# Query blocks of 512 columns with a 64-query remainder, in a relu²-attention and gated-FFN kernel

## Chip, cores and metric

The kernel runs on one core of one Trainium2 chip. The metric is device time in microseconds for one execution. Before the change the median of three runs is 1611.57 us (1611.5 to 1611.7).

## The reference

Four batches of 3136 rows go through an attention whose weights are the squared positive part of the scores, and then through a feed-forward block (FFN) with a three-tap convolution and a sigmoid gate. All arrays are float32; D is 256, the score depth 64, the hidden width 1024.

```python
scores = (1.0 / S) * z @ z.transpose(0, 2, 1)       # (4, 3136, 3136), symmetric
x = u * (np.maximum(scores, 0.0) ** 2 @ v)          # (4, 3136, 256)
h = np.maximum(x @ w_in, 0.0)                       # (4, 3136, 1024)
conv_out[:, t] = sum(conv_w[k] * hp[:, t + k] for k in range(3))   # hp: h with a zero row at each end
out = (h * sigmoid(conv_out)) @ w_out               # (4, 3136, 256)
```

## The kernel before

**Precision.** TensorE works on fp32r operands. To keep fp32 accuracy every operand is split into a rounded high part and the rest (hi and lo: `ah`/`al`, `vh`/`vl`, `gh`/`gl`, `xh`/`xl`, `wih`/`wil`, `woh`/`wol`). A product is three matmuls: lo weight by hi, hi weight by hi, hi weight by lo. For the scores hi and lo of 64 rows each fill the 128 rows of the array, so that two matmuls (`zhh` and `zll` against `zq`) do.

**Tiling.** A batch has 7 query blocks of `NB` = 448 columns (`QB` = 7), 28 blocks in all. The keys are 25 chunks of 128 rows (`NJ` = 25), the last of 64 rows. A block has 25 slots, one for each key chunk. In a slot `attend` (L348) issues 6 matmuls of 448 columns into two PSUM banks `av0` and `av1` (4 for the half chunk, the block's last slot), and `scores` (L256) 2 matmuls for a slot `LA` = 4 ahead. `relu`, `square`, `split_hi` and `split_lo` turn scores into `ah` and `al` on ScalarE and VectorE.

**Symmetry.** Scores of chunks that an earlier block has computed for other queries are not computed again. `part` (L279, GpSimd) and `spill` (L287) write them to DRAM as two halves of 16 bits; `fetch` (a transposing DMA on SyncE's queue) and `join` (L307, GpSimd) bring them back transposed. This replaces 277 of the 700 slots' scores.

**FFN.** After a block's attention `gate_x` (L367) takes `av0` and `av1` out of PSUM and multiplies by u, `split_x` makes hi and lo, and the FFN of that block runs inside the next block's slots, one of 8 hidden chunks every three or four slots (`FS`): 6 matmuls in (`ffn_in`), relu, three taps, sigmoid, gate and split on ScalarE, VectorE and GpSimd, and 6 matmuls out (`ffn_out`) some ten slots later. A block's last two output columns need the next block's first hidden row, so the tiles run one column late; `halo` carries two columns from block to block, and a batch's last block has 450 columns.

**Order.** The order on every engine is written out by hand: `ev[slot]` has six classes, and the loop at the end (L604) runs PRE, the attention's steps, POST, PE0, `attend`, `scores`, PE1. Tile releases make the semaphore waits. The last block's FFN has nothing beside it and has a schedule of its own (`T_S` to `T_L`, `last_block`, L564). The weights arrive as float64 and are turned to fp32 in blocks 0 to 2 (`prep_w`, mostly VectorE).

**PSUM** has 8 banks of 512 fp32 columns: `s` two, `ph` two, `av0`, `av1`, `o0`, `o1`. A query block of 448 leaves 64 columns of each empty.

Of the kernel before, what the change touches and what calls it, by code (L numbers as in the profile page):

```python
# [55 lines left out]
T_S, T_X = 3, 0  # L56
T_O = [1, 1, 2, 2, 3, 3, 4, 5]
T_C = [3, 3, 3, 1, 4, 2, 2, 0, 1]
T_H, T_L = "AAVAAVAA", "GVGVGVGV"


@with_exitstack
def kernel(
# [16 lines left out]
    NB = 448  # L80
    QB = S // NB
    NJ = (S + P - 1) // P
    HALF = S - (NJ - 1) * P
    NBLK = B * QB
# [5 lines left out]
    assert DC == 2 and KW == 3 and 2 * DQ == P and HALF == 64  # L90
# [20 lines left out]
    ent = [[entries(b, q) for q in range(QB)] for b in range(B)]
    assert all(e[-1] == (NJ - 1, False) for x in ent for e in x)
# [14 lines left out]
    halo = const.tile([P, FC, 2], F32, name="halo")  # L127
    ebias = const.tile([P, 1], F32, name="ebias")
# [11 lines left out]
    def load_z(b, q):  # L140
        t = wk.tile([P, NB], F32, tag="zt", name="zt")
        nc.sync.dma_start(out=t, in_=z[b, :, q * NB : (q + 1) * NB])
        zst[q] = t

    def prep_z(q):
        c, t = slice(q * NB, (q + 1) * NB), zst.pop(q)
        nc.scalar.copy(zhh[:, c], t)
        sub(nc.gpsimd, zll[:, c], t, zhh[:, c])
        if q == QB - 1:

            for x in (zhh, zll):
# [12 lines left out]
    def first_z():
        t, h = zst.pop(0), 256
        x = wk.tile([P, NB], F32R, tag="zq", name="zq")
        nc.scalar.copy(zhh[:, :NB], t)
        nc.scalar.copy(x[LO], t[LO])
        sub(nc.vector, x[HI], t[HI], zhh[HI, :NB])
        sub(nc.vector, zll[:, :h], t[:, :h], zhh[:, :h])  # L170
        sub(nc.gpsimd, zll[:, h:NB], t[:, h:], zhh[:, h:NB])
        zq[0] = x
# [83 lines left out]
    def scores(k):  # L256
# [10 lines left out]
        nc.tensor.matmul(s[:, :NB], lhsT=zhh[:, w], rhs=zq[blk], start=True, stop=False)  # L267
        nc.tensor.matmul(s[:, :NB], lhsT=zll[:, w], rhs=zq[blk], start=False, stop=True)  # L268
# [406 lines left out]
```

## Time and the profile before

| What | Value |
|---|---|
| median of the runs | 1611.57 us |
| the profiled execution: span, first to last instruction | 1609.6 us |
| TensorE matmul (PE) busy | 1582.4 us (98%), 7678 matmuls |
| weight loads (PEld) busy | 1437.5 us (89%) |
| ScalarE (ACT) busy | 1272.6 us (79%) |
| VectorE (DVE) busy | 1145.3 us (71%) |
| GpSimd (POOL) busy | 1100.5 us (68%) |
| granted TensorE clock, mean | 1.000 of full speed |
| DMA | 179.66 MB, mean 112 GB/s |

The page gives no time for the profiled execution other than its span; what lies around the span (launch and end) is the difference to the median, 2.0 us. Durations of matmuls overlap, because they are pipelined: a row's duration of 0.36 us is the way of one matmul through the array, and the pace is read from the starts. "Idle before" is the time an engine waited just ahead of a group, and the arrow names what ended it.

### The profile page before, as it was taken

Reading aid. Unit: us, or ns where it says so; the run is one execution under the profiler, and the core shown is the slowest. Engines: PE = TensorE matmul, PEld = TensorE weight load, DVE = VectorE, ACT = ScalarE, POOL = GpSimd, SP = SyncE. Lnnn points to the kernel's source line nnn. Section 1 sums busy time; section 2 is a strip of 40 time slices with the busy share of each in tenths; the row PEclk is TensorE's granted clock in tenths of the full one; section 3 lists DMA queues with packets and bytes.
Section 4 is the critical chain, followed back from the end, with each engine's and each line's share of the span. In section 5 each row is a group of like instructions: output and inputs, shape, how many; then the busy total and the mean of one; then the engine's idle time right before and its main releaser. Section 6 shows DMA issues by size and latency. Waiting matters only on the chain.

```text
span 1609.6 us, 24946 instructions
## 1 busy us (share of the span) xinstructions
PE 1582.4 (98%) x7678; PEld 1437.5 (89%) x7678; DVE 1145.3 (71%) x1933; ACT 1272.6 (79%) x2592; POOL 1100.5 (68%) x1451
## 2 busy tenths in 40 slices
PE   8899999999999999999999999999999999999998
PEld 7678999999999989999999998999999999999997
DVE  7897776667777777666777767766677777666656
ACT  8888777888877778788877777787887777787886
POOL 6775567787856667678785666777877566677772
PEclk9999999999999999999999999999999999999999
DMA  5342244555434434556453344445634334444450
GB/s 175 120 127 78 78 124 116 113 110 131 148 89 112 113 94 113 122 112 125 103 159 95 95 129 103 108 112 115 148 102 128 98 98 112 110 104 102 117 103 23
DMA packets 371399, 179.66 MB, mean 112 GB/s; under 512 B 264897, under 2 KB 370241, under 8 KB 371265
## 3 DMA queue, kind: packets, MB, share of 16 engines
q1 hardware_dynamic: 371120, 177.84, 44.3%
q8 instruction: 60, 0.98, 0.3%
q14 instruction: 75, 0.61, 0.1%
q10 hardware_dynamic: 144, 0.23, 0.0%
HBM read 36.59 MB, written 77.87 MB: 71 GB/s over the span
## 4 chain that ended last, share of the span: by engine, by line
PE 87%; ACT 5%; DVE 4%; issue 2%; POOL 2%; DMA 0%; POOLq 0%; ACTq 0%; DVEq 0%
PE av L358 15%; PE av L359 15%; PE av L360 15%; PE ph L393 5%; PE ph L391 5%; PE s L267 5%; PE ph L392 5%; PE o L460 5%; PE o L458 5%; PE o L459 5%; PE s L268 5%; DVE al L131 1%; ACT t L319 1%; ACT xh L381 1%; DVE ph L427 1%
## 5 line engine op out<-in xcount | busy, mean ns | idle before, releaser
L131 DVE TENSOR_TENSOR al<-s,ah 128x448 fp32r<-128x448 f32 x672 | 418.3, 622 | 238.5 <-ACT ah L335 163.0
L358 PE MATMUL av<-ah,vl 128*128 128x448 f32 x1344 | 492.7, 367 | 3.4 <-ACT ah L337 2.4
L360 PE MATMUL av<-al,vh 128*128 128x448 f32 x1344 | 491.7, 366 | 1.7 <-DVE al L131 1.4
L359 PE MATMUL av<-ah,vh 128*128 128x448 f32 x1344 | 492.3, 366 | 0.0
L330 DVE TENSOR_TENSOR s<-s,t 128x448 f32<-128x448 f32 x396 | 249.7, 630 | 205.2 <-ACT t L319 204.9
L311 POOL COPY tj<-tp 128x896 uint16<-128x896 uint16 x277 | 335.4, 1214 | 2.1 <-DMA tp<-dq 2.1
L319 ACT ACTIVATE t<-s 128x448 f32<-128x448 f32 x423 | 230.5, 545 | 116.8 <-PE s L268 106.4
L337 ACT CAST ah<-s 128x448 fp32r<-128x448 f32 x423 | 225.6, 533 | 112.0 <-DVE s L330 110.2
L427 DVE SCALAR_TENSOR_TENSOR ph<-hb,cw,ph 128x448 f32<-128x448 f32 (+1 forms) x448 | 304.8, 681 | 3.3 <-POOL gl L131 1.9
L131 POOL TENSOR_TENSOR gl<-c,gh 128x448 fp32r<-128x448 f32 (+1 forms) x220 | 255.6, 1162 | 67.9 <-ACT gh L134 63.2
L285 POOL COPY pl<-t 128x896 uint16<-128x896 uint16 x301 | 279.1, 936 | 1.4 <-ACT t L319 1.4
L358 PEld LDWEIGHTS av<-ah,vl 128*128 128x128 f32 x1344 | 252.6, 188 | 28.4 <-ACT ah L337 3.4
L360 PEld LDWEIGHTS av<-al,vh 128*128 128x128 f32 x1344 | 252.6, 188 | 25.5 <-DVE al L131 4.6
L359 PEld LDWEIGHTS av<-ah,vh 128*128 128x128 f32 x1344 | 252.7, 188 | 20.2
L416 POOL COPY halo<-hb 128x2 f32<-128x2 f32 x192 | 36.9, 192 | 291.0 <-ACT hb L414 290.9
L267 PE MATMUL s<-zq,zhh 128*128 128x448 f32 x423 | 160.3, 379 | 15.5 <-DVE al L131 8.7
L391 PE MATMUL ph<-xh,wih 128*128 128x448 f32 x448 | 164.3, 367 | 1.1 <-DVE c L441 0.7
L460 PE MATMUL o<-gl,woh 128*128 128x448 f32 (+1 forms) x448 | 164.1, 366 | 0.9 <-POOL gl L131 0.9
L393 PE MATMUL ph<-xl,wih 128*128 128x448 f32 x448 | 164.2, 367 | 0.3 <-POOL hb L405 0.3
L458 PE MATMUL o<-gh,wol 128*128 128x448 f32 (+1 forms) x448 | 164.3, 367 | 0.0
L459 PE MATMUL o<-gh,woh 128*128 128x448 f32 (+1 forms) x448 | 164.0, 366 | 0.0
L392 PE MATMUL ph<-xh,wil 128*128 128x448 f32 x448 | 163.7, 365 | 0.0
(78 smaller groups left out, 2370.5 us busy)
## 6 DMA issues: line engine op xcount, KB each, us to landing
dq<-pl SPq DMA_DIRECT2D x243, 224.0 KB, 2.3
ut<-in_u_dram SPq DMA_DIRECT2D x28, 448.0 KB, 3.8
vst<-in_v_dram SPq DMA_DIRECT2D x48, 256.0 KB, 3.1
dq<-pl SPq DMA_DIRECT2D x81, 112.0 KB, 2.4
out_dram<-ob SPq DMA_DIRECT2D x20, 448.0 KB, 3.3
zt<-in_z_dram SPq DMA_DIRECT2D x28, 224.0 KB, 3.1
tp<-dq SPq DMA_TRANSPOSE x277, 3.2
wr<-in_moe_w_in_dram SPq DMA_DIRECT2D x8, 256.0 KB, 3.2
```

The costliest lines, as they stand in the source:

```text
L131: eng.tensor_tensor(out=out, in0=a, in1=b.bitcast(F32), op=ALU.subtract)
L285: nc.gpsimd.tensor_copy(pl[k], rl.pop(k).bitcast(U16).rearrange("p (n h) -> p h n", h=2))
L311: nc.gpsimd.tensor_copy(tj[k].bitcast(U16).rearrange("p (n h) -> p h n", h=2), t)
L319: nc.scalar.activation(rl[k], sc[k][:, :NB], AF.Relu, scale=SC1)
L330: nc.vector.tensor_tensor(out=s, in0=s, in1=rl[k], op=ALU.mult)
L358: nc.tensor.matmul(o, lhsT=vl[:, j, d], rhs=h, start=first, stop=False)
L359: nc.tensor.matmul(o, lhsT=vh[:, j, d], rhs=h, start=False, stop=False)
L360: nc.tensor.matmul(o, lhsT=vh[:, j, d], rhs=l, start=False, stop=False)
L391: nc.tensor.matmul(o, lhsT=wih[:, dc, w], rhs=xh[blk][:, dc], start=(dc == 0), stop=False)
L393: nc.tensor.matmul(o, lhsT=wih[:, dc, w], rhs=xl[blk][:, dc], start=False, stop=(dc == DC - 1))
L427: nc.vector.scalar_tensor_tensor(out=c, in0=hb[blk, f][:, k : e + k], scalar=cw[:, f, k : k + 1], in1=c, op0=ALU.mult, op1=ALU.add,)
L458: nc.tensor.matmul(o, lhsT=wol[:, f, d], rhs=h, start=(f == 0), stop=False)
```

## The change

The query block becomes 512 columns, a whole PSUM bank. A batch then has 6 blocks (`QB` = 6) and 64 remaining queries (`RQ`), and the kernel 24 blocks.

- **The remainder's attention.** Hi and lo of 64 queries' attention weights stand side by side as one stationary operand of 128 columns, and `vv` (hi and lo of v side by side, 512 columns) streams past it: one matmul for each key chunk, 25 for a batch, in place of a query-block's six. It stands at the start of a batch's last block (`rem_attend`), in bank `av0`. `rem_evac` splits the result, `rem_turn` turns it to the transposed layout and adds the four products with 8 matmuls by a 0/1 matrix `pick`, and `rem_gate` multiplies by u into `xr`.
- **The remainder's scores** come for 20 chunks from DRAM (three transposing DMAs, `rem_fetch`, and `rem_join`), and for the last 5 chunks from 10 matmuls of 64 columns (`rem_scores`).
- **The remainder's FFN** is one tile of 4 × 64 columns (with seams, 266 in the output) for all four batches, at the kernel's end, its 8 hidden chunks interleaved with those of the last block (`jobs`, `T_M`, `T_R`). The last hidden chunks of the block before (`T_P`) go there as well.
- **The queries' tile goes.** `za` holds hi in rows 0 to 63 and lo in rows 64 to 127, `zb` the other way round; a column range of `za` is the moving operand itself, and `queries` (two VectorE copies a block) is dropped. `prep_z` now takes four instructions on 64 rows (ScalarE, VectorE, two GpSimd) in place of two on 128.
- **Smaller moves.** The half chunk is a block's first slot, not its last (except in the first block); a block's first `attend` starts with `av1`; the gated product is written over `hb`; the staging tiles of z and v share four buffers; chunk bounds and block bounds now agree, so that a spilled chunk goes to one place.

```diff
-    NB = 448
+    NB = 512
     QB = S // NB
+    RQ = S - QB * NB
+    RB = QB - 1
...
         cs, ts = list(range(m)) + list(range(n, NJ)), list(range(m, n))
+        if b or q:
+            cs.insert(0, cs.pop())
...
-        nc.scalar.copy(zhh[:, c], t)
-        sub(nc.gpsimd, zll[:, c], t, zhh[:, c])
+        copy(e0, za[LO, c], t[LO])
+        copy(e1, zb[HI, c], t[HI])
+        sub(e2, zb[LO, c], t[LO], za[LO, c])
+        sub(e3, za[HI, c], t[HI], zb[HI, c])
...
-        nc.tensor.matmul(s[:, :NB], lhsT=zhh[:, w], rhs=zq[blk], start=True, stop=False)
-        nc.tensor.matmul(s[:, :NB], lhsT=zll[:, w], rhs=zq[blk], start=False, stop=True)
+        r = za[:, blk % QB * NB : (blk % QB + 1) * NB]
+        nc.tensor.matmul(s, lhsT=za[:, w], rhs=r, start=True, stop=False)
+        nc.tensor.matmul(s, lhsT=zb[:, w], rhs=r, start=False, stop=True)
...
+        for dc in reversed(range(DC)) if first else range(DC):
...
+    def rem_split(i):
+        t = rs.pop(i).rearrange("p (c n) -> p c n", n=RQ)
+        a = rr["a"][:, RN[i][0] : RN[i][-1] + 1]
+        nc.scalar.copy(a[:, :, 0], t)
+        sub(nc.gpsimd, a[:, :, 1], t, a[:, :, 0])
+
+    def rem_attend():
+        rr["o"] = o = ps.tile([P, 512], F32, tag="av0", name="av0")
+        for j in range(NJ):
+            n = slice(0, min(P, S - j * P))
+            nc.tensor.matmul(
+                o,
+                lhsT=rr["a"][n, j].rearrange("p h n -> p (h n)"),
+                rhs=vv[n, j].rearrange("p h d -> p (h d)"),
+                start=j == 0,
+                stop=j == NJ - 1,
+            )
+
+    def rem_evac():
+        o, a = rr.pop("o"), rr.pop("a").rearrange("p c h n -> p (c h n)")
+        rr["h"], rr["l"] = h, l = a[:, :NB], a[:, NB : 2 * NB]
+        nc.scalar.copy(h, o)
+        sub(nc.vector, l, o, h)
+
+    def rem_turn():
+        h, l = rr.pop("h"), rr.pop("l")
+        rr["t"] = p = ps.tile([P, 512], F32, tag="ph", name="ph", bufs=2)
         for dc in range(DC):
+            ops = [w[:, c * P : (c + 1) * P] for w in (h, l) for c in (dc, DC + dc)]
+            for i, w in enumerate(ops):
+                nc.tensor.matmul(
+                    p[:, dc * RQ : (dc + 1) * RQ], lhsT=w, rhs=pick, start=i == 0, stop=i == len(ops) - 1
+                )
...
-    for blk in range(1, NBLK):
-        at(blk * NJ - LA - 2, VEC, queries, blk)
+    for b in range(B):
+        k5 = (b * QB + RB) * NJ
...
+        at(k5 + R_D, PE1, rem_scores, n)
...
+        at(k5 + 1, PRE, rem_evac)
+        at(k5 + R_T, PE1, rem_turn)
+        at(k5 + R_T + 1, VEC, rem_gate, b)
...
+        at(NS - 2, POST, rem_x)
+        jobs = [(NS + T_M[f], blk, f, "ph", "av") for f in range(FC)]
+        jobs += [(NS + T_R[f], "r", f, "s", "o") for f in range(FC)]
...
+            if rem:
+                rem_attend()
+                if k + LA < NS:
+                    scores(k + LA)
+                run(e[PE1])
             if 0 <= k < NS:
                 attend(k)
```

## Rows read from the trace of the kernel before

**Rows 1.** The page: busy time, share of the span and instructions of each engine.

```profile
PE 1582.4 (98%) x7678; PEld 1437.5 (89%) x7678; DVE 1145.3 (71%) x1933; ACT 1272.6 (79%) x2592; POOL 1100.5 (68%) x1451
```

**Rows 2.** Busy time by stretch: first two blocks, middle, a last block, blocks 8, 27's FFN.

```profile
core 0: us, PE busy (x) PEld busy (x) DVE busy (x) ACT busy (x) POOL busy (x), PEclk, DMA share, GB/s
4.70:57.60 52.90, 48.06 (x206) 38.72 (x206) 43.31 (x75) 45.21 (x101) 41.37 (x45) 1.00 0.54 165
57.60:121.90 64.30, 58.20 (x271) 49.96 (x271) 56.84 (x102) 55.76 (x124) 43.20 (x61) 1.00 0.40 118
121.90:1525.30 1403.40, 1397.88 (x6826) 1279.02 (x6827) 989.76 (x1667) 1107.22 (x2242) 971.18 (x1274) 1.00 0.45 112
...
345.40:399.20 53.80, 53.33 (x262) 48.67 (x261) 36.31 (x61) 46.15 (x95) 43.21 (x53) 1.00 0.57 133
...
459.10:518.30 59.20, 59.20 (x292) 54.39 (x291) 43.73 (x76) 43.89 (x88) 35.52 (x50) 1.00 0.40 110
...
1576.40:1605.60 29.20, 27.20 (x128) 23.18 (x127) 22.66 (x38) 21.36 (x42) 8.63 (x23) 1.00 0.04 17
```

**Rows 3.** Instructions grouped by line and shape: attend and scores on TensorE.

```profile
L358 PE MATMUL av<-ah,vl 128*128 128x448 f32 x1344 | 492.7, 367 | 3.4 <-ACT ah L337 2.4 <-DVE ut L369 0.9
...
L268 PE MATMUL s<-zq,zll 128*128 128x448 f32 x423 | 155.8, 368 | 0.6 <-POOL zll L131 0.6
```

**Rows 4.** TensorE in order of time, among the first matmuls: start, duration, instruction.

```profile
5.85 0.57 PE L267 MATMUL s<-zq,zhh 128*128 128x448 f32 x1
...
7.34 0.57 PE L267 MATMUL s<-zq,zhh 128*128 128x448 f32 x1
```

**Rows 5.** In order of time near 757 us: matmuls and one late weight load.

```profile
757.29 0.36 PE L360 MATMUL av<-al,vh 128*128 128x448 f32 x1
757.38 0.19 PEld L267 LDWEIGHTS s<-zq,zhh 128*128 128x128 f32 x1
...
757.49 0.37 PE L267 MATMUL s<-zq,zhh 128*128 128x448 f32 x1
...
757.70 0.37 PE L268 MATMUL s<-zq,zll 128*128 128x448 f32 x1
```

**Rows 6.** In order of time near 187 us: a later weight load, and the next.

```profile
187.07 0.37 PE L360 MATMUL av<-al,vh 128*128 128x448 f32 x1
...
187.21 0.19 PEld L267 LDWEIGHTS s<-zq,zhh 128*128 128x128 f32 x1 [0.15 <-DVE al L131]
...
187.32 0.19 PEld L268 LDWEIGHTS s<-zq,zll 128*128 128x128 f32 x1
```

**Rows 7.** Groups by line and shape on the other engines: widths 256 to 512.

```profile
L134 ACT CAST vh<-vst 128x512 fp32r<-128x512 f32 x47 | 29.1, 620 | 0.1
...
L134 ACT CAST gh<-c 128x448 fp32r<-128x448 f32 x192 | 107.3, 559 | 0.7 <-PE ph L393 0.7
...
L131 POOL TENSOR_TENSOR vl<-vst,vh 128x512 fp32r<-128x512 f32 x48 | 62.2, 1295 | 19.3 <-ACT vh L134 18.5 <-DVE vh L134 0.7
...
L131 POOL TENSOR_TENSOR gl<-c,gh 128x448 fp32r<-128x448 f32 x192 | 223.0, 1162 | 46.7 <-ACT gh L134 43.2 <-DVE wm L231 2.6
...
L131 DVE TENSOR_TENSOR al<-s,ah 128x448 fp32r<-128x448 f32 x672 | 418.3, 622 | 238.5 <-ACT ah L335 163.0 <-ACT ah L337 63.1 <-PE av L359 3.5
...
L233 DVE TENSOR_TENSOR wm<-wm 128x256 f32<-128x256 f32 x1 | 0.4, 409 | 0.0
```

**Rows 8.** The same view: the query copies on VectorE.

```profile
L161 DVE CAST zq<-zll 64x448 fp32r<-64x448 f32 x27 | 14.9, 551 | 0.4
L160 DVE CAST zq<-zhh 64x448 fp32r<-64x448 f32 x27 | 13.3, 494 | 0.0
```

**Rows 9.** TensorE's waits over the run: total us, times, longest.

```profile
PE s L267 <- DVE al L131: 8.7, 17, 1.6
```

**Rows 10.** In order of time, the end: the last matmul and the last DMA issue.

```profile
1605.56 0.37 PE L460 MATMUL o<-gl,woh 128*128 128x450 f32 x1
...
1606.63 0.37 ACTq L483 DMA_DIRECT2D out_dram<-ob  x1
```

More of the change, by code (lines that the diff above doesn't have):

```diff
@@ L164, in first_z @@
-    def first_z():
[L165 to L172, printed above, removed]
+        t = wk.tile([P, NB], F32, tag="st", name="st", bufs=4)
+        w = min(NB, S - q * NB)
+        nc.sync.dma_start(out=t[:, :w], in_=z[b, :, q * NB : q * NB + w])
@@ L349, in attend @@
         blk, j, _ = at_slot(k)
-        first = k % NJ == 0
+        first, last = k % NJ == 0, k % NJ == NJ - 1
         if first:
@@ L365 @@
-    xh, xl = {}, {}
+        for dc in reversed(range(DC)) if first else range(DC):
+            o = pav[blk][dc]
+            d = slice(dc * P, (dc + 1) * P)
+            ops = [(vl, h), (vh, h)] + ([(vh, l)] if l is not None else [])
+            for i, (w, r) in enumerate(ops):
+                nc.tensor.matmul(
+                    o, lhsT=w[:, j, d], rhs=r, start=first and i == 0, stop=last and i == len(ops) - 1
+                )
+    rt, rs, rr = {}, {}, {}
+    RN = [range(i * CB, min(i + 2, RB) * CB) for i in range(0, RB, 2)] + [range(RB * CB, NJ)]
@@ new lines, in rem_picks, with rem_u @@
+    def rem_picks():
+        t = wk.tile([P, RQ], F32, tag="tj", name="pk", bufs=3)
+        nc.gpsimd.memset(t, 0.0)
+        for base in (0, -RQ):
+            nc.gpsimd.affine_select(
+                out=t, in_=t, pattern=[[-1, RQ]], compare_op=ALU.not_equal, fill=1.0, base=base, channel_multiplier=1
+            )
+        nc.vector.tensor_copy(pick, t)
+    def rem_u(b):
+        t = wk.tile([P, DC, RQ], F32, tag="ur", name="ur", bufs=1)
+        nc.sync.dma_start(out=t, in_=u[b, :, QB * NB : S].rearrange("(a p) s -> p a s", p=P))
+        rr["u"] = t
@@ new lines, in rem_scores, with rem_relu @@
+    def rem_scores(i):
+        p = ps.tile([P, 512], F32, tag="ph", name="ph", bufs=2)
+        r = za[:, QB * NB : S]
+        for x, j in enumerate(RN[i]):
+            w, o = slice(j * P, (j + 1) * P), p[:, x * RQ : (x + 1) * RQ]
+            nc.tensor.matmul(o, lhsT=za[:, w], rhs=r, start=True, stop=False)
+            nc.tensor.matmul(o, lhsT=zb[:, w], rhs=r, start=False, stop=True)
+        rr["p"] = p
+    def rem_relu(i):
+        n = len(RN[i]) * RQ
+        rs[i] = t = wk.tile([P, NB], F32, tag="t", name="rj", bufs=3)[:, :n]
+        nc.scalar.activation(t, rr.pop("p")[:, :n], AF.Relu, scale=SC1)
@@ L480, in evac @@
                 nc.scalar.copy(r[:, dc, :e], o[dc][:, :e])
-            if end:
-                dst, src = outs(blk)
-                (nc.scalar if dc else nc.sync).dma_start(out=dst[:, dc], in_=src[:, dc])
+        if end:
+            for dst, src in outs(blk):
+                for dc in range(DC):
+                    (nc.scalar if dc else nc.sync).dma_start(out=dst[:, dc], in_=src[:, dc])
     def store(blk):
-        dst, src = outs(blk)
-        nc.sync.dma_start(out=dst, in_=src)
+        for dst, src in outs(blk):
+            nc.sync.dma_start(out=dst, in_=src)
     ev = defaultdict(lambda: tuple([] for _ in range(6)))
@@ L499, in at @@
         ev[slot][cls].append((fn, args))
-    for q in range(2, QB):
-        s = (7 * q) // 2 - LA - 2
+    for q in range(2, QB + 1):
+        s = 4 * q - LA - 3 if q < QB else 4 * QB - LA - 4
         at(max(s - 4, -LA), POST, load_z, 0, q)
@@ L546 @@
         at(k0 + XS, C_XS, split_x, blk, (G, G))
+        ahead = blk == NBLK - 2
         for f in range(FC):
```

280 lines of the change are left out of this document (182 added, 98 removed).

## Prediction

> **What bounds the kernel.** I read the page first: TensorE (PE) is busy for 98% of the span, the next engine for 79% [rows 1]. Then the busy time by stretch, which shows where the idle rest lies [rows 2]. In block 8 (459.1 to 518.3 us) PE never stands idle, and 291 matmuls (the 292 shown, less one cut at the edges) take 59.2 us: 203.4 ns from start to start. That is the pace of a 448-column matmul with nothing in its way. A group's mean of 367 ns [rows 3] is one matmul's way through the array and no price.
>
> With this pace I part each stretch into matmuls and stalls [rows 2]. Blocks 0 and 1: 52.9 − 206 × 0.2034 = 11.0 us and 64.3 − 271 × 0.2034 = 9.2 us of stalls. The 25 blocks up to 1525 us: 1403.4 − 6826 × 0.2034 = 15.0 us, 0.6 each. The last FFN: 29.2 − 128 × 0.2034 = 3.2 us. The whole: the first matmul starts at 4.7 us, 7678 × 0.2034 = 1561.7 us of matmuls, 38.6 us of stalls (0.2 in the last attention), and 4.0 us from the last matmul's start to the end of the span [rows 10]: 1609.0 us, 0.6 short of the span of 1609.6. The median of the runs lies 2.0 us above that span.
>
> So only three things can move the time: how many matmuls there are, what one costs, and the stalls, half of which lie in the first two blocks.
>
> **What sets a matmul's price.** Either its columns, or the weight load ahead of it. The rows that decide are those where a load came late [rows 5]. The load for L267 began at 757.38, 0.09 us after the matmul ahead of it had started at 757.29, because it waited; yet L267 started at 757.49, 0.20 us after that matmul, as ever. A load that starts 90 ns late costs nothing, so the load isn't the pace. Near 187 us the load came 0.14 us late, and the next load followed 0.11 us behind it [rows 6]: 0.11 us is what a load needs. The pace is thus the matmul's own streaming, and 512 columns will cost more than 448.
>
> How much more, no row shows, since nearly all matmuls have 448 columns. The first matmuls, right after PE's idle start, follow one another at (7.34 − 5.85) / 4 = 0.3725 us [rows 4]. That is 448 columns at the lower clock level of 1.2 GHz (373.3 ns) with nothing on top. At 2.4 GHz, the granted clock of all later stretches (1.00 [rows 2]), the columns take 186.7 ns, and 16.7 ns of the 203.4 are something else. Below: if the 16.7 ns vanish in longer streaming, 512 columns cost 213.3 ns. Above: if they grow with the columns, 203.4 × 512 / 448 = 232.5 ns. I take a fixed 16.7 ns, 230.0 ns. Each ns here is 6.7 us of the result, and this is the largest unknown.
>
> The Trainium skill ("TensorE: Matmul & The Clock Gate", section "Wait — 56ns, not 53.3ns?") has a fixed surcharge too, of about 2.5 ns at the full clock: 189.2 ns for 448 columns, where the rows here give 203.4. By its 215.7 ns for 512 columns the matmuls below would take an estimated 96 us less. The measured pace speaks against its size.
>
> **The matmuls, before and after.** Before: 28 blocks × (24 × 6 + 4 in the attention + 96 in the FFN) = 6832, and 423 × 2 for scores: 7678, as on the page. After: 24 × 244 = 5856 in the blocks. Chunks taken from DRAM are 0, 4, 8, 12, 16, 20 for a batch's blocks, but 0, 0, 4, 8, 16, 20 in batch 0, 228 of 600 slots, so 372 × 2 = 744 for scores. The remainder's attention is 4 × 25 = 100, also of 512 columns. Together 6700 × 0.2300 = 1541.0 us. The remainder's FFN: 48 of 256 columns, (256 / 2.4 + 16.7) = 123.4 ns each, 5.9 us, and 48 of 266, 127.5 ns, 6.1 us; both are longer than a load's 110 ns, so the load stays hidden. Then 72 matmuls of 64 columns (10 scores and 8 turns a batch), which would stream faster than their weights load: 0.11 us each, 7.9 us. Sum 1560.9 us, against 1561.7 before. **The gain of 978 fewer wide matmuls is nearly eaten:** they carry 6700 × 512 = 3.43 million columns, as the 7678 × 448 = 3.44 million did, and the narrow matmuls cost 20 us for 30 thousand columns.
>
> **The stalls.** Blocks 0 and 1 are held by the other engines: DVE is busy 43.3 of 52.9 us and 56.8 of 64.3 us, ACT 45.2 and 55.8 [rows 2]. Wider tiles cost these engines slightly less per column: from 448 to 512 columns ACT goes from 559 to 620 ns, POOL from 1162 to 1295 (× 1.11 each), DVE by the slope (622 − 409) / 192 to about 693 [rows 7], × 1.11, where PE goes × 1.131. The weights' preparation does not grow at all. VectorE loses the two query copies, 0.55 + 0.49 us a block [rows 8], and gains a half-height copy for each z block instead. GpSimd pays more: `prep_z` has two subtractions where it had one, each about as long as a full one, some 6 us more in block 0, where POOL has 11 us free. The first chunk that needs the second z block is number 4, not 3. I take 9 us for block 0 and 6 for block 1 (from 5 to 20 together with what may go wrong up to 25). The 21 middle blocks keep 0.6 us each, 12.6 us; much of that is the wait of scores for VectorE at a block's change [rows 9]. In a batch's last block ACT has 46.2 us for 53.8 and POOL 43.2 [rows 2]; after it both have 1.11 times that, and PE 1.13 plus the remainder's 5.8, so neither becomes the bound.
>
> **The remainder's waits.** `rem_split` ends some three slots ahead, so `rem_attend` finds its operand. Its bank `av0` is wanted again by the first `attend`, which must wait for `rem_evac`: an ACT copy (0.62) and a DVE subtraction (0.69) behind the last of the 25 matmuls, about 1.8 us with the way through the array (0.37) and the handovers. Beside it run that last matmul, two scores and two matmuls into `av1`, 5 × 0.23 = 1.15 us. Left 0.7 us, four times: 2.8 us (0 if more covers it, 6 if the copy queues on ACT). Nothing else queues behind the wait on PE but the following slots. While PE streams the 25, ACT and DVE run out of scores after about four slots and lose nothing that PE waits for, since the splits of the next two slots are by then done.
>
> **The two ends.** The first z tile has 512 columns: first matmul at 5.0 us. At the end the last FFN has 16 interleaved jobs, 24 outs of the block before fill the gap after `gate_x`; VectorE's share there was 22.7 of 29.2 us already [rows 2], and main and remainder jobs need about 4.2 us of DVE for 4.3 us of PE: I take 5 us of stalls (3 to 10) with the last attention's. The remainder's output goes out in eight DMAs, four on each of two queues, with 0.37 us an issue [rows 10]: 5.2 us from the last matmul to the end, not 4.0.
>
> **Sum.** 5.0 + 1560.9 + 9 + 6 + 12.6 + 2.8 + 5 + 5.2 = 1606.5 us, 2.5 less than the 1609.0 that the same sum gives before. Off the span: 1607.1; with the 2.0 us around it **1609 us**. About 0.2% (3.2 us) is what a measurement of this kernel can tell from no change, and this lies inside it.
>
> **The rivals.**
> 1. *The excess grows with the columns* (232.5 ns): a moving operand that arrives a little slower than 2.4 GHz would do this, and explain too why the lower clock shows no excess. 6700 × 2.5 ns = 17 us more: 1626, slower. It decides from 230.7 ns on; up to there the fewer matmuls pay for the narrow ones.
> 2. *Load and stream share a path* (partly hidden excess): 448 + 128 columns would take the 203.4 ns, and 512 + 128 then 226.0. 27 us less: 1582. For it: no excess at the lower clock, where there is time for both.
> 3. *A floor under the pace:* 203.4 would be a fixed time beside the streaming, and 512 columns cost 213.3: 112 us less, 1497. Against it stand the late loads [rows 5], which rule out the load as that floor. The Trainium skill's surcharge (same section) would end near this, at an estimated 1513.
> 4. *The remainder starves PE.* If the four slots of lead don't outlast 25 matmuls without scores, PE waits afterwards for most of them: 4 × 5 us, 1629. Against it: ACT and DVE have 10 to 30% to spare in these blocks.
>
> **How the numbers follow.** Fixed excess 0.50: 1609, within ±9 from the stalls' bounds and a pace of 228.8 to 231.2 (its halves: faster 0.23, same 0.16, slower 0.11). Rival 1 0.17, rival 2 0.20, rival 3 0.05, rival 4 0.08. Faster 0.23 + 0.20 + 0.05 = 0.48, slower 0.11 + 0.17 + 0.07 = 0.35, same 0.17 with a hundredth of rival 4. The range, 1578 to 1628, leaves out rival 3 and the outer ends of 2 and 4.
>
> **What would show it.** Right: groups of 128x512 matmuls, 6700 in all, and a stretch without stalls at 0.230 us each; 96 matmuls of 256 and 266 columns some 0.125 us apart; four runs of 25 with less than 1 us idle behind each; the first two blocks with some 15 us of stalls. Wrong: a pace below 0.228 or above 0.232, whatever the stalls; an idle PE for several us after a run of 25; GpSimd near its full time in blocks 0 or 5; a last FFN that takes over 42 us from its `gate_x`.

## The result, and the profile after

The changed kernel takes 1626.28 us (median; 1623.86 to 1630.57), the kernel before 1611.53 beside it: ratio 1.0094, 95% interval 1.0078 to 1.0110, slower by some 15 us. The forecast was 1609, about no change. The profiled execution took 1626.88 us with a span of 1624.8.

The page of the changed kernel, busy time of each engine, answers to [rows 1]:

```profile
PE 1578.1 (97%) x6868; PEld 1277.0 (79%) x6868; DVE 1133.4 (70%) x1712; ACT 1232.6 (76%) x2299; POOL 1106.9 (68%) x1320
```

TensorE is still the busiest. The busy time by stretch (columns as in [rows 2]) says where it isn't: block 0, block 1, block 4 of batch 0, two blocks of batch 1 for the pace, and everything from the last `gate_x` on. The last four rows are short stretches around two moments at which the granted clock changed.

```profile
5.15:66.90 61.75, 54.90 (x207) 39.12 (x207) 50.19 (x79) 49.16 (x101) 48.89 (x52) 1.00 0.46 139
66.90:139.30 72.40, 66.79 (x275) 51.95 (x275) 59.41 (x102) 60.92 (x125) 44.25 (x59) 0.98 0.37 110
266.90:333.10 66.20, 61.02 (x269) 49.21 (x268) 44.42 (x66) 49.99 (x95) 55.40 (x60) 1.00 0.47 113
401.20:533.20 132.00, 132.00 (x579) 108.29 (x578) 98.58 (x148) 99.50 (x183) 89.45 (x108) 1.00 0.40 116
1558.80:1624.80 66.00, 48.06 (x225) 36.65 (x223) 40.76 (x70) 35.70 (x73) 16.12 (x45) 0.95 0.07 21
95.00:99.30 4.30, 2.48 (x11) 1.75 (x10) 4.30 (x7) 2.91 (x6) 3.12 (x4) 1.00 0.47 141
99.30:102.70 3.40, 3.40 (x9) 2.65 (x9) 2.86 (x7) 2.27 (x5) 2.23 (x4) 0.50 0.48 134
1567.00:1570.40 3.40, 1.09 (x8) 0.84 (x6) 2.86 (x4) 1.69 (x4) 0.28 (x3) 1.00 0.00 0
1570.40:1573.80 3.40, 3.35 (x9) 2.77 (x10) 1.93 (x4) 2.48 (x6) 1.28 (x1) 0.50 0.00 0
```

Three things are to be read here. Up to the last `gate_x` the change gains: it falls at 1558.8 us, where it fell at 1576.4 before [rows 2], 17.6 us earlier. From there to the end it loses more: 66.0 us, where it was 33.2 before (1576.4 to 1609.6). Of these 32.8 us more, 11.6 are the remainder's 96 narrow matmuls, which were meant to lie there, 3.2 the longer pace of the 127 wide ones, 2.4 the end, and 15.7 are stalls (18.9 against 3.2). And in those 66 us no engine is full: TensorE is busy for 48.1, VectorE for 40.8, ScalarE for 35.7, GpSimd for 16.1.

In 401.20 to 533.20 us TensorE never stands idle, and 578 matmuls (the 579 shown, less one cut at the edges) take 132.0 us, 228.4 ns each. Over all 512-column matmuls of the run that did not stall, from start to start, the mean is 228.9 ns.

Instructions grouped by line and shape, for the number of matmuls (answers to [rows 3]):

```profile
L380 PE MATMUL av<-ah,vv 128*128 128x512 f32 x2400 | 742.5, 392 | 6.6 <-DVE ar L144 3.0 <-ACT ah L358 2.4 <-ACT x L490 0.8
...
L586 PE MATMUL o<-al,woh 128*128 128x266 f32 x16 | 4.9, 308 | 0.9 <-DVE al L144 0.6 <-POOL al L144 0.3
...
L515 PE MATMUL ph<-xr,wih 128*128 128x256 f32 x16 | 4.6, 289 | 0.0
...
L465 PE MATMUL ph<-pick,ar 128*128 128x64 f32 x32 | 3.9, 266 | 0.0
```

All such groups together hold 6700 matmuls of 512 columns, 48 of 256, 48 of 266 and 72 of 64, as forecast. From start to start the 256- and 266-column ones take some 119 and 122 ns, the 64-column ones 102 on average.

TensorE in order of time, near the start and behind the last `gate_x` (answers to [rows 4]):

```profile
5.75 0.63 PE L289 MATMUL s<-za,zb 128*128 128x512 f32 x1
...
6.60 0.63 PE L289 MATMUL s<-za,zb 128*128 128x512 f32 x1
...
1559.23 0.39 PE L515 MATMUL ph<-xh,wih 128*128 128x512 f32 x1
...
1560.59 0.40 PE L584 MATMUL o<-gh,wol 128*128 128x512 f32 x1
...
1562.47 0.40 PE L586 MATMUL o<-gl,woh 128*128 128x512 f32 x1
```

At the start two matmuls take 0.85 us, 0.425 each: 512 columns at 1.2 GHz (426.7 ns) and nothing on top. The granted clock of that stretch reads 1.00; that it is the lower level is concluded from the same pace, some 427 ns, in the row 99.30 to 102.70, where it reads 0.50. Later six `ffn_in` matmuls take 1.36 us, 0.227 each, and eight outs 1.88 us, 0.235 each.

TensorE's waits from the last `gate_x` to the last matmul (what waited, for what; us in total, times, longest). There are five kinds above 1 us, where the last FFN before had 3.2 us of stalls in all [rows 2]:

```profile
PE o L586 <- POOL gl L144: 2.9, 4, 1.0
PE o L584 <- ACT gh L147: 2.5, 4, 1.7
PE ph L515 <- DVE hb L567: 2.4, 1, 2.4
PE o L584 <- DVE gh L147: 1.3, 2, 1.0
PE o L586 <- DVE gl L144: 1.1, 3, 0.4
```

The list gives idle time, 11.8 us with its smaller kinds. From start to start each of these 18 waits costs some 0.27 us more than the engine's idle time, and nine matmuls at half the clock cost 1.6: together these are nearly all of the 18.6 to 18.9 us of stalls spoken of below.

The outs wait for their gated values again and again (`gh`, `gl`), and once `ffn_in` waits for a bank. One round of it, in order of time (an idle time and who ended it stand in brackets):

```profile
1594.87 0.39 PE L517 MATMUL ph<-xl,wih 128*128 128x512 f32 x1
...
1595.34 0.58 ACT L560 ACTIVATE ph<-ph 128x512 f32<-128x512 f32 x1 [1.30 <-DVE ph L553]
...
1597.42 0.51 PE L584 MATMUL o<-gh,wol 128*128 128x512 f32 x1 [0.26 <-ACT gh L147]
...
1597.90 0.38 ACT L560 ACTIVATE ph<-ph 128x266 f32<-128x266 f32 x1 [0.53 <-DVE ph L553]
1598.18 0.59 ACT L541 ACTIVATE hb<-ph 128x512 f32<-128x512 f32 x1
...
1598.77 0.50 PE L586 MATMUL o<-gl,woh 128*128 128x512 f32 x1 [0.62 <-POOL gl L144]
...
1603.81 0.51 PE L584 MATMUL o<-gh,wol 128*128 128x512 f32 x1 [1.01 <-DVE gh L147]
```

A main job's `ph` is complete at 1595.26 (1594.87 + 0.39), but its relu (L541) starts at 1598.18, 2.9 us later. It stands on ScalarE behind two sigmoids (L560), each of which waits for VectorE's second convolution step of its own job, 1.30 and 0.53 us. The first wait ended at 1595.34, when the relu had only just become ready; so of the 2.9 us ScalarE idles for some 0.6 while a relu that could run stands in its queue, and for the rest it works on steps that stand ahead of it. Then the chain of that job is late: its outs begin at 1603.81, 1.01 us after TensorE fell idle.

The end, last matmul and the last groups of DMA issues (answers to [rows 10]):

```profile
1617.92 3.38 SPq L620 DMA_DIRECT2D out_dram<-ob  x5
...
1618.40 0.28 PE L586 MATMUL o<-al,woh 128*128 128x266 f32 x1
...
1619.19 1.81 ACTq L620 DMA_DIRECT2D out_dram<-ob  x4
```

From the last matmul's start to the end of the span it is 6.4 us, of which 3.5 lie behind the last issue, SyncE's (1617.92 + 3.38 = 1621.30, to 1624.8).

### The profile page after: what moved, and what is told of

The parts are those of the page before. It is cut to its first block, busy times and chain, and to the rows that moved or that the text cites. A ratio compares the mean times of both kernels' runs of the same rounds, so it can differ in the third digit from the quotient of the medians.

```text
span 1624.8 us, 22336 instructions
## 1 busy us (share of the span) xinstructions
PE 1578.1 (97%) x6868; PEld 1277.0 (79%) x6868; DVE 1133.4 (70%) x1712; ACT 1232.6 (76%) x2299; POOL 1106.9 (68%) x1320
## 4 chain that ended last, share of the span: by engine, by line
PE 80%; ACT 7%; DVE 5%; POOL 4%; issue 3%; DMA 1%; SPq 0%; ACTq 0%; POOLq 0%; DVEq 0%
PE av L380 41%; PE ph L517 5%; PE ph L515 5%; PE ph L516 5%; PE o L586 5%; PE o L584 5%; PE o L585 5%; PE s L288 5%; PE s L289 4%; DVE ph L553 2%; PE av L445 1%; POOL tj L332 1%; ACT t L340 1%; ACT ph L548 1%; DVE al L144 1%
## 5 line engine op out<-in xcount | busy, mean ns | idle before, releaser
L380 PE MATMUL av<-ah,vv 128*128 128x512 f32 x2400 | 742.5, 392 | 6.6 <-DVE ar L144 3.0
L144 DVE TENSOR_TENSOR al<-s,ah 128x512 fp32r<-128x512 f32 x576 | 397.2, 690 | 220.5 <-ACT ah L356 158.5
L380 PEld LDWEIGHTS av<-ah,vv 128*128 128x128 f32 x2400 | 449.5, 188 | 113.5 <-DVE ar L144 4.7
L380 PE MATMUL av<-al,vv 128*128 128x512 f32 x1152 | 451.7, 392 | 3.7 <-DVE al L144 3.4
L351 DVE TENSOR_TENSOR s<-s,t 128x512 f32<-128x512 f32 x345 | 240.6, 697 | 182.2 <-ACT t L340 180.3
L340 ACT ACTIVATE t<-s 128x512 f32<-128x512 f32 x372 | 222.6, 598 | 115.7 <-PE s L289 102.4
L332 POOL COPY tj<-tp 128x1024 uint16<-128x1024 uint16 x228 | 307.9, 1360 | 0.4
L553 DVE SCALAR_TENSOR_TENSOR ph<-hb,cw,ph 128x512 f32<-128x512 f32 x384 | 286.8, 747 | 12.5 <-ACT ph L548 11.9
L144 POOL TENSOR_TENSOR gl<-hb,gh 128x512 fp32r<-128x512 f32 x188 | 243.4, 1294 | 59.2 <-ACT gh L147 54.8
L308 POOL COPY pl<-t 128x1024 uint16<-128x1024 uint16 x248 | 259.1, 1050 | 9.0 <-DMA dq<-pl 8.6
L380 PEld LDWEIGHTS av<-al,vv 128*128 128x128 f32 x1152 | 216.6, 188 | 54.0 <-DVE al L144 9.1
L288 PE MATMUL s<-za 128*128 128x512 f32 x372 | 148.0, 398 | 18.2 <-DVE al L144 12.6
L584 PE MATMUL o<-gh,wol 128*128 128x512 f32 x384 | 153.4, 399 | 3.7 <-ACT gh L147 2.5
L560 ACT ACTIVATE ph<-ph 128x512 f32<-128x512 f32 x200 | 115.6, 578 | 54.6 <-DVE ph L553 48.6
L586 PE MATMUL o<-gl,woh 128*128 128x512 f32 x384 | 153.0, 399 | 4.1 <-POOL gl L144 2.9
```

The lines of the kernel that those rows point to most:

```text
L144: eng.tensor_tensor(out=out, in0=a, in1=b.bitcast(F32), op=ALU.subtract)
L308: nc.gpsimd.tensor_copy(pl[k], rl.pop(k).bitcast(U16).rearrange("p (n h) -> p h n", h=2))
L332: nc.gpsimd.tensor_copy(tj[k].bitcast(U16).rearrange("p (n h) -> p h n", h=2), t)
L340: nc.scalar.activation(rl[k], sc[k][:, :NB], AF.Relu, scale=SC1)
L351: nc.vector.tensor_tensor(out=s, in0=s, in1=rl[k], op=ALU.mult)
L380: nc.tensor.matmul(o, lhsT=w[:, j, d], rhs=r, start=first and i == 0, stop=last and i == len(ops) - 1)
```

## The experiments

Theory after the result, the **ring**: the last FFN is held by its own cycle of chain, lead and banks, not by any engine's share. Rivals: that it is plain work; that the time is lost in the first blocks and in batch 0's block 4. All kernels are edits of the changed one. In the table, the last FFN is the time from the last `gate_x` to the end of the span, and its stalls are the starts on TensorE that came later than the pace, summed from the order of time of each trace (one execution of each kernel; matmuls at half the clock count as late). Four traces whose last FFN is the same code (changed, e2, e4, e12) have 18.6 to 19.7 us of stalls there: that is how far one execution differs from another. Ratios are to the kernel before on the same chip.

| kernel | median us | ratio, 95% interval | last FFN us | its stalls us | block 4, batch 0: stalls us |
|---|---|---|---|---|---|
| changed | 1626.28 | 1.0094 [1.0078, 1.0110] | 66.1 | 18.6 | 6.1 |
| e1_tail_order | 1620.88 | 1.0059 [1.0043, 1.0075] | 59.0 | 11.9 | 8.9 |
| e2_pick_late | 1625.45 | 1.0088 [1.0072, 1.0104] | 65.9 | 19.7 | 8.9 |
| e3_no_remainder_ffn | 1618.66 | 1.0045 [1.0029, 1.0061] | 57.2 | 23.1 | 6.0 |
| e4_gpsimd_relief | 1622.61 | 1.0071 [1.0052, 1.0089] | 66.1 | 19.2 | 0.4 |
| e5_combined | 1612.60 | 1.0005 [0.9996, 1.0014] | 59.2 | 11.7 | 1.2 |
| e6_banks | 1608.35 | 0.9977 [0.9968, 0.9986] | 56.1 | 8.8 | 0.4 |
| e7_gpsimd_hi | 1608.05 | 0.9977 [0.9967, 0.9987] | 54.2 | 6.6 | 0.4 |
| e8_rem_bank | 1608.06 | 0.9978 [0.9969, 0.9987] | 55.4 | 6.7 | 1.2 |
| e9_tail_ends | 1606.20 | 0.9965 [0.9951, 0.9978] | 53.7 | 6.4 | 0.6 |
| e10_lead | 1626.73 | 1.0092 [1.0078, 1.0106] | 65.4 | 18.7 | 6.2 |
| e11_order | 1629.66 | 1.0110 [1.0096, 1.0124] | 69.0 | 22.4 | 8.9 |
| e12_split | 1628.59 | 1.0103 [1.0089, 1.0117] | 66.1 | 19.2 | 7.7 |

**The order and the lead together (e1).** The chain's later steps move to later slots, so that a sigmoid no longer follows its convolution in the same slot, and the outs come one slot later.

```
-T_O = [1, 1, 1, 2, 2, 2, 3, 3]
-T_C = [3, 3, 3, 3, 1, 1, 2, 1, 2]
+T_O = [1, 1, 2, 2, 3, 3, 4, 4]
+T_C = [3, 3, 3, 1, 1, 1, 2, 1, 2]
...
-            o = s + 4 if w != "r" else max(s + 4, NS + T_RO)
+            o = s + 5 if w != "r" else max(s + 5, NS + T_RO)
```

> The last FFN's jobs are staged one slot deeper: sigmoid one slot after the second tap instead of in the same slot, outs five slots after ins instead of four. Same work. Theory (a ring through two in-order queues: a job's sigmoid waits for the taps of the same slot, the next job's relu stands behind that sigmoid on ScalarE, and its taps behind the relu, 5.9 us for a main job and a remainder job together against 4.2 us of matmuls): the ring opens, a pair takes about 4.5 us, 8 pairs save 11 us: 1612 to 1619 us, stalls in the last FFN down from 18.6 to about 8 us. Rival (the last FFN is bound by the amount of work on VectorE and TensorE): under 2 us, 1624 to 1628 us.

It came out between the two ranges, 5.4 us below the changed kernel, and the last FFN is 7.1 us shorter with the same matmuls. So it is not plain work, but the ring is not gone either. TensorE's waits in this last FFN are now others:

```profile
PE ph L515 <- DVE hb L567: 3.1, 1, 3.1
PE ph L515 <- DVE gl L144: 2.5, 3, 0.9
PE o L586 <- POOL gl L144: 1.2, 1, 1.2
```

The outs' waits are nearly gone; what remains is `ffn_in` waiting for a bank of `ph`. Part of the gain went elsewhere in this execution: block 4 of batch 0 had 8.9 us of stalls, not 6.1, though e1 does not touch that block. The two waits in it are nearly the same, but in e1 the granted clock fell to one half behind each of them. The 3.4 us from one us behind the first wait on, in the changed kernel and then in e1:

```profile
289.70:293.10 3.40, 3.40 (x16) 2.77 (x15) 2.51 (x4) 2.46 (x6) 1.89 (x3) 1.00 1.05 292
```

```profile
290.10:293.50 3.40, 3.40 (x9) 2.64 (x8) 2.54 (x4) 2.45 (x6) 1.85 (x3) 0.50 1.06 259
```

TensorE is busy in all of both, but gets through 16 matmuls in one and 9 in the other. So in the table 6.0 to 6.2 is this block without a fall of the clock (changed, e3, e10), and 8.9 with two (e1, e2, e11).

**Each half of it alone (e10, e11).** e10 keeps only the `o = s + 5` line of that diff, e11 only the two lists.

> Of e1 only the outs one slot later, the order of the other steps as in the changed kernel. If the short lead of the outs over their gated values is what makes the stalls: most of e1's gain, 1620 to 1622.5 us, with the last FFN some 6 us shorter. If the order on ScalarE and VectorE makes them: 1625 to 1628.

> Of e1 only the order of the steps (second half of the chain spread over more slots), the outs as early as in the changed kernel. If the lead matters: no gain or a loss, since the high and low parts then come in the same slot as the outs that want them: 1626 to 1632 us. If the order matters: 1620 to 1622.5.

e10 gained nothing (1626.73; 18.7 us of stalls in its last FFN), against the expectation from the lead; e11 came out 3.4 us slower, as the lead's side of it had said. The intervals of e11 and the changed kernel overlap, and two falls of the clock in block 4 are part of the difference; what shows its loss is 22.4 us of stalls in the last FFN. The waits of e10's last FFN tell why:

```profile
PE ph L515 <- DVE gl L144: 5.4, 2, 3.1
PE ph L515 <- DVE hb L567: 2.4, 1, 2.4
PE o L584 <- ACT gh L147: 1.7, 1, 1.7
```

The wait has moved. With later outs the outs wait less, but the main jobs have only two banks of `ph`, and job f + 2 waits until job f gives its bank back: at the gate, or, in every second job, after VectorE has taken the low part out of the bank (`gl`, L144). With a later chain and the old lead (e11) the outs wait longer. Neither the order nor the lead is the cause by itself; three limits lie one behind the other.

**The remainder's FFN left out (e3).** The eight remainder jobs and their output are not computed; the main jobs and their slots stay.

```
-        jobs += [(NS + T_R[f], "r", f, "s", "o") for f in range(FC)]
```

> The eight remainder jobs of the last FFN and their output are left out; the main jobs stay in their slots. Theory (ring): the ring then holds main jobs alone, about 3.7 us each, and 8 times 2.2 us go, with 1 us of output DMAs: 17 to 20 us less, 1606 to 1609 us. Rival (work): the 96 narrow matmuls take 11.5 us and the output 1 us: 12 to 13 us less, 1613 to 1614 us.

Both missed: 1618.66. The last FFN lost 11.6 us of matmuls but only 8.9 us of time: its stalls grew to 23.1 us, and the end is 1.7 us shorter. From its waits:

```profile
PE o L584 <- ACT gh L147: 6.1, 3, 2.3
PE o L586 <- POOL gl L144: 3.4, 4, 1.4
PE ph L515 <- DVE hb L567: 3.1, 1, 3.1
```

The remainder jobs are cover as well as load. In the changed kernel TensorE has, between a main job's `ffn_in` and its outs, the outs of one main job and the `ffn_in` of the next (six matmuls each, 1.4 us each), and of the remainder two `ffn_in` and two outs (0.7 us each): 5.7 us. Without the remainder 2.8 us are left, while the chain of a main job is at least relu 0.59, tap 0.69, two steps 1.54, sigmoid 0.58, gate 0.69, cast 0.62 and 1.27 for GpSimd's low part, 6.0 us without a handover. This agrees with the ring, but not with the size that I had given it.

**The start and the middle (e2, e4, e12).** e2 moves the making of the pick matrix from before the loop to slot 70. e4 moves the preparation of batch 1's first two z blocks to slots 95 and 79, and takes the remainder's low parts on VectorE. e12 does only the latter.

```
-        rem_picks()                                     # before the loop          (e2)
+    at(70, POST, rem_picks)                             #                          (e2)
...
-                s = (Q0 - QB) * NJ + NJ + k0 + 4 + 8 * q  #                        (e4)
+                s = (Q0 - QB) * NJ + k0 + 20 - 16 * q     #                        (e4)
...
-        sub(nc.gpsimd, a[:, :, 1], t, a[:, :, 0])       # in rem_split        (e4, e12)
+        sub(nc.vector, a[:, :, 1], t, a[:, :, 0])       #                     (e4, e12)
```

> The 0/1 matrix is made at slot 70 instead of ahead of the loop. Theory (VectorE's copy of it waits for GpSimd until 9.3 us, and the first squares, the first attention matmuls and the rise of the clock wait behind it): 3 to 4 us less, 1622 to 1623.5 us, and the first attention matmul at 8.5 us instead of 10.7. Rival (blocks 0 and 1 are held by VectorE's and ScalarE's work, and what is won early is lost a few slots later): under 1 us.

> The two z blocks of the second batch that are prepared in block 4 are prepared in block 3, and the remainder's subtractions go from GpSimd to VectorE. Theory (in block 4 GpSimd falls behind, VectorE stands behind its late joins, and the scores wait): of the stalls of 6.1, 1.2, 1.9 and 1.1 us in the four blocks 4 some 5 to 7 us go: 1619 to 1621 us. Rival (VectorE only takes over the delay): under 2 us.

> Of e4 only the remainder's low parts on VectorE, the z blocks' preparation where the changed kernel has it. If GpSimd's queue as a whole is late in batch 0's block 4, each relief helps: stall there 2 to 4 us instead of 6.1, 1622.5 to 1625 us. If the two z blocks falling together are the cause, it stays at 5 to 6 us, 1625 to 1627; if the split alone is, it falls below 1 us.

In e2 the first attention matmul came at 8.7 us, close to the 8.5 expected, and the first two blocks became 1.9 and 1.6 us shorter (59.9 and 70.8 us). Only the first of these is the pick matrix. Block 1 of the changed kernel has a fall of the clock, at 99.3 us; e2 has the same stretch ahead of it, with the same 11 matmuls, and no fall:

```profile
93.30:97.60 4.30, 2.48 (x11) 1.75 (x10) 4.15 (x6) 2.91 (x7) 2.85 (x4) 1.00 0.45 145
```

e4 and e10 have no fall there either, though they leave the pick matrix where it was. In all traces without that fall block 1 has 8.1 or 8.2 us of stalls, in those with it (changed, e1, e3, e11, e12) some 9.7. Batch 0's block 4, which e2 does not touch, came out longer, with two falls of the clock. The median fell by 0.8 only, which is the rival's figure and a miss for the theory.

e4's block 4 of batch 0 is without waits; TensorE's busy time in that stretch of e4 is the whole of it:

```profile
266.10:326.20 60.10, 60.10 (x268) 48.99 (x267) 44.75 (x68) 48.66 (x93) 50.62 (x54) 1.00 0.59 126
```

It took 6 us less than in the changed kernel; the median fell by 3.7 us, short of the range expected by 1.6. e12 gave nothing there (stalls of 7.7 us, of which one fall of the clock is 1.5, and a median above all three of its ranges): of e4's two edits the place of the z blocks is the one that works. That edit alone was not run.

**Put together, and the banks (e5, e6).** e5 is e1, e2 and e4 in one. e6 lets main and remainder jobs alternate between the two pairs of banks and takes all low parts on GpSimd, whose input is then not the bank:

```
-T_H, T_L = "AAVAAVAA", "GVGVGVGV"
+T_H, T_L = "AAVAAVAA", "GGGGGGGG"
...
-        jobs = [(NS + T_M[f], blk, f, "ph", "av") for f in range(FC)]
-        jobs += [(NS + T_R[f], "r", f, "s", "o") for f in range(FC)]
+        jobs = [(NS + T_M[f], blk, f, ("ph", "s")[f % 2], "av") for f in range(FC)]
+        jobs += [(NS + T_R[f], "r", f, ("s", "ph")[f % 2], "o") for f in range(FC)]
```

> The tail's order of e1, the late pick of e2 and the GpSimd relief of e4 together. If the three waits are separate, their gains add: 5.4, 0.8 and 3.7 us below the changed kernel's 1626.3, and some 1 to 3 us more since e2 lost in batch 0's block 4 what e4 gives there: 1613 to 1616 us, still slower than before. Rival (one stall stands in for another, and any stall of over 2 us costs a clock fall as well): 1617 to 1621.

> e5 with the tail's PSUM banks used otherwise: main and remainder jobs alternate between the two pairs of banks, so that main job 1 needs no bank of the block before, and all low parts are taken on GpSimd, so that a bank is free at the gate. In e1 the waits for banks were 3.3 us at main job 1, with 1.6 us of half clock behind it, and three of 1.0 us. If banks are what is left: 6 to 9 us below e5, 1605 to 1610, faster than before. If the in-order queues of ScalarE and VectorE bind instead: within 2 us of e5.

e5 reached 1612.60, a little better than its best case: none of the three gains stands in for another, and together the edits give more than their sum (13.7 us against 9.9). The surplus fits the falls of the clock in block 4, two in the traces of e1 and e2 and none in e5, where the z blocks' place has taken the waits away; that the other executions had them too is not shown. Nor does a stall of over 2 us always cost a fall, as the rival had it: the changed kernel's two in block 4 did not. e6 is 4.3 us below e5, faster than before, though less than the 6 to 9 expected: the three waits of 1.0 us for banks are gone, but that at main job 1 (3.3 us in e5) came back as 1.9 us at the second remainder job, which now wants the bank that the block before still holds. The waits for banks, as idle time, in e5 and then in e6:

```profile
PE ph L515 <- DVE hb L567: 3.1, 1, 3.1
PE ph L515 <- DVE gl L144: 2.5, 3, 0.9
```

```profile
PE ph L515 <- DVE hb L567: 1.8, 1, 1.8
```

Of e6's two edits, the pairs of banks and the low parts on GpSimd, neither was run alone. In e6 the granted clock also fell for 6.8 us behind these stalls; e8 has the same stalls and no fall. The two rows of e6, and then the same two stretches of e8:

```profile
1559.00:1562.50 3.50, 1.75 (x9) 1.15 (x8) 3.43 (x7) 2.36 (x5) 0.00 (x0) 1.00 0.01 2
1562.50:1569.30 6.80, 6.06 (x17) 4.50 (x17) 3.60 (x7) 4.90 (x11) 3.76 (x7) 0.50 0.08 30
```

```profile
1561.00:1564.50 3.50, 1.76 (x9) 1.14 (x8) 3.43 (x7) 2.36 (x5) 0.00 (x0) 1.00 0.01 2
1564.50:1571.30 6.80, 5.34 (x27) 4.19 (x27) 3.74 (x8) 6.27 (x14) 4.20 (x10) 1.00 0.08 30
```

**ScalarE's share, and the remainder's bank (e7, e8).** e7 casts the remainder's high parts on GpSimd; e8 accumulates the remainder's attention in a bank of `ph`. Both stand on e6.

```
-            at(h, T_C[7], ffn_hi, w, f, E[T_H[f]])
+            at(h, T_C[7], ffn_hi, w, f, G if w == "r" else E[T_H[f]])      # e7
...
-        rr["o"] = o = ps.tile([P, 512], F32, tag="av0", name="av0")
+        rr["o"] = o = ps.tile([P, 512], F32, tag="ph", name="ph", bufs=2)  # e8
```

> e6 with the high parts of the remainder's gated values cast on GpSimd, not on ScalarE or VectorE. By the changed kernel's durations ScalarE has some 4.15 us of work for a pair of jobs where TensorE has some 4.2. If ScalarE binds the tail of e6: 2 to 3 us below e6. If it doesn't: within 0.7 us of it, or above by the longer GpSimd chain.

> e6 with the remainder's attention accumulated in a bank of ph, not in av0, so that the first attend of a batch's last block needn't wait for the remainder's evacuation. If that wait is what it seems (0.91 us behind each run of 25, four times): 3 to 4 us below e6, and block 5 without the stall on VectorE's subtraction. If the wait only moves to the next user of ph: within 1 us of e6.

Neither moved the median (1608.05 and 1608.06 against 1608.35). So ScalarE's share does not bind. In e8 the 0.91 us behind each run of 25 are gone, but 0.64 us ahead of it have come (the run's bank is still held by the last chunk of the block before, until its gate): the wait only moved, as the rival said. Three of these four waits, as idle time of TensorE:

```profile
PE ph L445 <- DVE hb L567: 1.4, 3, 0.5
```

**Both ends of the last FFN (e9).** On e7: the second half of `xl` on GpSimd, and four DMAs for the remainder's output instead of eight.

```
-        at(NS + T_X, T_C[0], split_x, blk, (V, V))
+        at(NS + T_X, T_C[0], split_x, blk, (V, G))
...
-            for dst, src in outs(blk):
+            for i, (dst, src) in enumerate(outs(blk)):
+                if blk == "r":
+                    (nc.scalar if i % 2 else nc.sync).dma_start(out=dst, in_=src)
+                    continue
```

> e7 with two more edits at the ends of the last FFN: the low part of its second half of x on GpSimd, so that VectorE comes 1.1 us earlier to the last chunk of the block before, whose bank a remainder job waits for (1.9 us in e7); and the remainder's output in four DMAs, two a queue, not eight. If VectorE's order holds the bank, that wait falls to about 0.8 us, and the end from the last matmul by 0.7 us (two issues of 0.37 us a queue fewer): 1605.5 to 1607. Rival (the first low parts then wait for GpSimd, and the end is the last transfer's own way): within 0.5 us of e7's 1608.05.

1606.20, in the range, the fastest of all and 0.35% below the kernel before. The wait on `hb` fell from 1.7 to 1.3 us only, as idle time, so most of the 1.1 us expected did not come. VectorE was free earlier, but then idled longer for a tap on ScalarE (L548), which stands behind a relu that waits for `ffn_in`. VectorE's convolution steps, and with them the gate behind them that frees the bank, in e7 and then in e9:

```profile
1559.09 2.21 DVE L553 SCALAR_TENSOR_TENSOR ph<-hb,cw,ph 128x512 f32<-128x512 f32 x3 [1.44 <-ACT ph L548]
```

```profile
1559.38 2.21 DVE L553 SCALAR_TENSOR_TENSOR ph<-hb,cw,ph 128x512 f32<-128x512 f32 x3 [2.00 <-ACT ph L548]
```

The last issue ends 2.1 us behind the last matmul's start, in e7 3.1; but what follows it took 4.1 us, in e7 3.3, so the end is 6.2 us, where it was 6.4. The median fell by 1.9 us in all, within the spread of e7's runs (1606.37 to 1610.45), and the intervals of the two ratios overlap, so that e9 is faster than e7 is not shown. But in its last FFN a stretch of 26 us, 146 matmuls long, now runs without a stall, VectorE and ScalarE at 80 and 78%:

```profile
1566.50:1592.50 26.00, 26.00 (x146) 22.59 (x147) 20.70 (x39) 20.39 (x42) 18.14 (x43) 1.00 0.06 21
```

## Why the prediction was wrong, step by step

The sum of the prediction beside what the profiled execution gave (a stretch less its matmuls at 228.9 ns and at the narrow prices is its stalls):

| term | forecast us | measured us |
|---|---|---|
| first matmul | 5.0 | 5.15 |
| 6700 matmuls of 512 columns | 1541.0 | 1533.6 |
| the remainder's FFN, 96 matmuls | 12.0 | 11.6 |
| 72 narrow matmuls | 7.9 | 7.4 |
| stalls, block 0 | 9 | 14.4 |
| stalls, block 1 | 6 | 9.6 |
| stalls, middle, with the remainder's waits | 15.4 | 17.7 |
| stalls, last FFN | 5 (3 to 10) | 18.9 |
| end | 5.2 | 6.4 |
| sum | 1606.5 | 1624.8 |

- **The pace came out near the forecast, but its reason only in part.** 228.9 ns against 230.0, which gave 7.4 us more than forecast. But 228.9 is a mean of two paces: 227 in most groups, 13.7 ns over streaming at 2.4 GHz, and 235 in the outs, 21.7 over it. Neither has the 16.7 of 448 columns, and 227 lies below the 0.228 us that the prediction named as a sign of being wrong; that the mean falls so close to 230.0 is partly luck. What the runs show is an excess that neither vanishes nor grows with the columns: 12 and 11 ns at 256 and 266 columns (119 and 122 ns), 14 to 22 at 512, and again none at the lower clock. By the prediction's terms the last `gate_x` falls at some 1555 us (6573 of the wide matmuls lie ahead of it); 1558.8 was measured.
- **Rival 1 met the time and is wrong all the same.** It had 1626, but by a pace of 232.5 ns; the pace is 228.9 on average, and 227 in five of six matmuls. (Its 230.7 for the turning point comes out of no sum of the prediction; its own total, 2.5 us below the kernel before at 6.7 us for each ns, gives 230.4.) Rival 2's 226.0 is only 1 ns from that 227, so the wide matmuls alone do not rule it out; but by its rule 256 + 128 columns would take 135.6 ns, and 119 were measured, and it has no place for the outs' 235. The floor of rival 3 is out: an excess that is still 13.7 ns or more at 512 columns is no floor. Rival 4 did not come: behind the four runs of 25 `attend` waits 3.0 us in all for the remainder's low part (`ar` in the group of L380 above), and all stalls of a block 5 are 1.5 us, where the prediction had 0.7 and 0.6.
- **The step that failed** is the one on the two ends: "main and remainder jobs need about 4.2 us of DVE for 4.3 us of PE: I take 5 us of stalls (3 to 10)". It weighed engines by their share and never laid the cycle out: how long a main job's chain is, how much TensorE has to do between its `ffn_in` and its outs (5.7 us against a chain of 6.0 and more), on how many banks, and in which order ScalarE takes the steps. Measured 18.9 us, beyond the bound of 10, and 13.9 of the 18.3 us by which the sum is off. e1, e10 and e11 show the chain and the lead as limits one behind the other, and e1's and e6's waits the banks as the next; with all three eased, e9 has 6.4 us, near the value that was assumed.
- **The bound that should have warned** was there: the prediction named "a last FFN that takes over 42 us" as a falsifier, but its own terms add to about 50 (24 outs 5.5, 96 matmuls 22.1, the remainder 12.0, stalls 5, end 5.2). The stretch was never summed by itself.
- **The first two blocks** were mis-sized by 9.0 us together, 24.0 against 15, inside the bounds named (5 to 20, up to 25). Some 1.4 us of it is the pick matrix, made ahead of the loop: block 0 has 13.8 to 15.0 us of stalls in the seven traces with it there, 12.6 to 13.8 in the six without. Another 1.5 us is the fall of the clock in block 1. The rest of the excess was not taken apart.
- **Batch 0's block 4** is 5.5 of the 17.7 us of the middle: GpSimd is busy for 55.4 of its 66.2 us, two z blocks are prepared in it, and scores wait twice on VectorE for it, 2.4 and 2.8 us. The prediction looked at GpSimd's share in blocks 0 and 5 and not at 4. e4 shows that the place of the z blocks is what matters there.
- **The end** is 1.2 us longer than forecast in this execution. Among the kernels with the same eight issues it is 5.2 (e2) to 7.5 us (e8), so the term is not shown to be wrong, and e9's 6.2 us with four lies within that spread.

What stays open: the rest of the first two blocks' stalls; and what decides whether the clock falls behind a stall.

## What to carry to other kernels

Price a pipelined tail by its cycle, not by its engines' shares: the length of one job's chain with its handovers, against what the matrix engine has to do between the job's input and its output, and against the time after which its bank is wanted again; and look in each in-order queue for a step that waits in front of one that could run. Such limits lie one behind another: easing one may show nothing, or a loss (e10, e11), and easing them all shows what each was worth. A job that is added can be cover as well as load, so leaving it out does not tell its price (e3).

## What the runs showed of the hardware that was not expected

- **The granted clock fell to one half in the middle of the run, for 3.4 us at a time**, at 99.3 and 1570.4 us of the changed kernel, each time behind a stretch in which TensorE had been busy for 2.5 of 4.3 us and 1.1 of 3.4 us. Before, the clock is 1.00 in every stretch after the start [rows 2]. At half the clock a 512-column matmul takes 427 ns, and in blocks 1 and 4 a fall of 3.4 us behind a stall costs some 1.5 us more than the stall. It need not come: e6 and e8 have the same stalls at the same place, and the fall came in one of them alone; so it is with the changed kernel and e2 in block 1, and with the changed kernel and e1 in block 4. The falls thus make one execution of the same block differ from another by 1.5 us (block 1) and 2.8 us (block 4). The kernels with such stalls also spread more from run to run: the changed kernel over 6.7 us in four runs, the kernel before over 0.3 in the four beside it and 2.5 in the 31 beside e5 to e8. In e11 the two runs of 1631.7 and 1631.8 us have mean granted clocks of 0.992 and 0.993, the two of 1627.5 and 1627.6 have 0.995. In the changed kernel's four runs time and clock do not line up, so the falls are not the whole of the spread.
- **Two paces for 512 columns**: outs of the FFN (L584 to L586) follow one another at some 235 ns, scores, attention and `ffn_in` at some 227. With 448 and 450 columns the groups did not differ like this. In the last FFN of the changed kernel, where the main jobs' outs go into `av0` and `av1`, they keep 233 to 235 ns, and there `ffn_in` too takes 230 to 233. So the banks `o0` and `o1` are not the cause, which stays open.
